# Three fused layers on one core: V's conversion, a second square tile, and the order of loads at a product's border

## The chip, the cores and the metric

The kernel runs on one core of a Trainium2 chip. Its engines are TensorE (PE, matmuls and weight loads), VectorE (DVE), ScalarE (ACT), GpSimd (POOL) and SyncE (SP, which here issues all DMA transfers). The metric is device time in microseconds (us). An engine executes its own instructions in order and waits on semaphores for the others.

## The reference

Three layers follow each other on 8 batches of 576 tokens with 512 channels.

```python
kv  = einsum('bhsd,bhse->bhde', k, v)            # attention without softmax, 8 heads of 64
out = einsum('bhsd,bhde->bhse', q, kv)
x   = out / sqrt(mean(out*out, -1) + 1e-6) * g_norm

u = x + (x^T @ U @ V)^T                          # U: 576 x 32, V: 32 x 576 (mixes tokens)
z = u + relu(u @ w_ch1) @ w_ch2                  # 512 -> 2048 -> 512

h = gelu(z @ w_in)                               # 512 -> 1024, halves hu and hv
result = z + (hu * (w_sg @ layernorm(hv) + b_sg)) @ w_out
```

The weights U, V, w_ch1, w_ch2, w_in and w_out arrive as 64-bit floats, and the kernel converts them on the chip.

## The kernel before, in words

**Numbers.** Products of the second and third layer run on fp32r halves: each operand is split into a high and a low part (`wh`, `wl`), and `three` (lines 346 to 349) issues three matmuls for one product. `convert` (lines 96 to 109) turns a 64-bit weight into fp32: two steps on ACT (lines 103, 104), three on DVE (106 to 108), one addition on POOL (109). These steps are marked `behind`: they keep their place in the program's order on their engine. `converted` (113) writes down the conversion, then flushes a queue of stores, then queues the store of its own result. A store (`split_to`, 123) is a copy on ACT (125) and a subtraction (126), on DVE for even blocks and on POOL for odd ones. So the store of block f is written down behind the conversion of block f + 1, unless `flush()` is called before.

**Order.** PE's order is the order of the code. The other engines and SP get a fixed order when the program is built: the framework's planner takes what it thinks is ready, and among that what comes first in the code; so an instruction that isn't `behind` can be put ahead of earlier ones, loads far ahead.

**Stage 1, per batch** (b = 0 to 7). `att_kv` multiplies K and V of the heads into a PSUM tile `kvps` (tag "ar", 4 buffers shared with `xps` and `ups`), `put_kv` copies it to `kvbd`. `att_x` (264) makes chunk c of 128 tokens: matmuls into `xps`, on ACT a square into the tile `sq` (276; one buffer) and a copy to `xn` (277), on DVE a sum of squares (278). `att_root` (281) is ten small DVE steps for the reciprocal root over all five chunks. `att_norm` (289) scales a chunk on DVE (295) and splits it into `xh` (ACT, 300) and `xl` (DVE, 301). `att_t` (304) multiplies with U into `tp`. `att_u` (321), for each quarter d of the channels, transposes the chunks (334) and multiplies with V's tile `v4` (336), both into `ups`, then scales the result (338, 340), stores it to `ud` in DRAM and splits it into `uh` and `ul` (343, 344). `ch1` (353) is one unit of the first product: 12 matmuls for half of a weight block f of 128 columns; 12 units per batch for blocks 0 to 5, whose outputs go to `yd` in DRAM. The other ten blocks are computed later in stage 1b by a scheme with seven products for eight (`Unit`).

**The head** (lines 470 to 522) prepares batches 0 and 1: loads; U's conversion; V's conversion in two halves, each followed by `store_v` (375: a copy on ACT, 376, and a subtraction on POOL, 377) into `v4`; then `att_kv(0)`, the five `att_x(0)`, root, `att_kv(1)`, the norms of batch 0 with its `att_t` and the `att_x` of batch 1 in between, `split_w(0)` and `split_w(1)`; then `att_u(0)`, the root and norms of batch 1 and `split_w(2)`, `split_w(3)`. Large tiles named `spare` stand in slots that the later coefficient tiles `c0` to `c4` will take.

**The periods** (524 to 571) run a list of steps per batch: U is a unit of `ch1`, X `att_x` and T `att_t` and D `att_u` of the next batch, K `att_kv` of the one after that. K0 and K1 are followed by the loads of that batch's third and fourth pair (`load_kv`, 165; tile `kvm` has 2 buffers, so a load waits for the K that last read its buffer). The first batch has a list of its own, `FIRST`.

**Stage 1b and the border** (575 to 713, then 716 on). The seven-product scheme runs over tokens in five blocks. Towards its end `load_w2` (682) loads the converted blocks of w_ch2 from DRAM (`wd`): blocks 8 to 15 into slots 0 to 7, which are free early, blocks 0 to 7 into a new pool `wb`, which lies where the tiles of stage 1b were.

**Stage 2, the second product** (773 to 807). 72 steps; a step takes 256 of the 2048 hidden channels of 512 tokens: `load_y` (743) loads `yr` from `yd` (one DMA) and makes relu and its low part (`yx`: ACT 752, DVE 753), then `ch2` issues 24 matmuls. Steps start with blocks 8 to 15, then 0 to 7; the input of the first two steps was loaded earlier (`y_at`). `load_z1` loads a batch of u for the residual.

Of the kernel before, what the change touches and what calls it, by code (L numbers as in the profile page):

```python
# [12 lines left out]
F32 = mybir.dt.float32  # L13
# [9 lines left out]
B, H, S, D = 8, 8, 576, 64  # L23
# [3 lines left out]
P = 128  # L27
# [32 lines left out]
def tile_kernel(ctx: ExitStack, tc: tile.TileContext, kvm, kvr, qt, gcol, uv, w12,  # L60
# [21 lines left out]
    def in_turn(*chains):  # L82

        end = object()
        while chains:
            chains = [steps for steps in chains if next(steps, end) is not end]
# [9 lines left out]
    def convert(raw, tmp):  # L96

        low, high = raw[:, :, 0], raw[:, :, 1]
        t = tmp.bitcast(I32)
        behind(nc.scalar.activation(tmp, high.bitcast(F32), AF.Abs))
        behind(nc.scalar.activation(low, low.bitcast(U32), AF.Copy, scale=2.0 ** -29))
        yield
        yield behind(nc.vector.tensor_scalar(tmp, tmp, 2.0 ** -15, 122879.9921875, ALU.max, ALU.min))
        yield behind(nc.vector.tensor_scalar(t, t, 3, 0x3FFFFFF8, ALU.logical_shift_left, ALU.bitwise_and))
        yield behind(nc.vector.scalar_tensor_tensor(t, high, -0x40000000, t, ALU.bitwise_and, ALU.bitwise_or))  # L108
        yield behind(nc.gpsimd.tensor_add(t, t, low))  # L109
# [9 lines left out]
    def flush():  # L119
        while queue:  # L120
            queue.pop(0)()
# [28 lines left out]
    def slot(i, shape, dt, name):  # L150

        return px["wa" if i < 14 else "xa"].tile([P] + shape, dt, tag=f"s{i}", name=f"{name}{i}")
# [49 lines left out]
    def split_w(f):  # L202
        w = slot(f, [2, DM], F32R, "w")
        wh[f], wl[f] = w[:, 0], w[:, 1]
        sub = nc.gpsimd if f % 2 else nc.vector
        converted(w_raw.pop((f, 0)), next_tmp(), split_to(w[:, 0], w[:, 1], sub))
# [39 lines left out]
    def att_kv(b, ps):  # L246
        if ps[0] == 0:
            at_s["kv", b] = pm.tile([P, NP, D], F32, tag="ar", bufs=4, name="kvps")
        acc = at_s["kv", b]
        for p in ps:  # L250
            m, r = kv_t.pop((b, p))
            for c in range(NC):
                src = m[:, c] if c < 4 else r
                for j in range(2):
                    mm(acc[j * D:(j + 1) * D, p, :], src[:, j * D:(j + 1) * D],
                       src[:, P + j * D:P + (j + 1) * D], start=(c == 0), stop=(c == NC - 1))
# [7 lines left out]
    def att_x(b, c):  # L264

        n = rows(c)
        if c == 0:
            at_s["ss", b] = small(b, "ss", 0)
            nc.gpsimd.memset(at_s["ss", b][64:, 4], 1.0)
        ps = pm.tile([P, H, D], F32, tag="ar", bufs=4, name="xps")  # L270
        for p in range(NP):
            mm(ps[:n, 2 * p:2 * p + 2, :], q_t[b, p][:, c * P:c * P + n], kvbd[:, p, :],  # L272
               start=True, stop=True)
        xn = xn_of(b, c)
        sq = ap.tile([P, H, D], F32, tag="sq", name="sq")
        nc.scalar.activation(sq[:n], ps[:n], AF.Square)
        nc.scalar.activation(xn[:n], ps[:n], AF.Copy)
        nc.vector.tensor_reduce(at_s["ss", b][:n, c], sq[:n], AX.X, ALU.add)
        at_s["x", b, c] = xn

    def att_root(b):
        ss = at_s.pop(("ss", b))
        y, t = (small(b, n, i) for i, n in ((1, "ny"), (2, "nt")))
        a, y2, t2 = (i.rearrange("p w h -> p (w h)") for i in (ss, y, t))
        nc.vector.tensor_scalar(a, a, 1.0 / D, EPS, ALU.mult, ALU.add)
        in_turn(rsqrt(y2, t2, a))
        at_s["y", b] = y

    def att_norm(b, cs):

        y = at_s["y", b]
        for c in cs:
            n = rows(c)
            xn = at_s["x", b, c]
            nc.vector.tensor_tensor(xn[:n], xn[:n], y[:n, c].unsqueeze(2).to_broadcast([n, H, D]),
                                    ALU.mult)
            xf = xn.rearrange("p h d -> p (h d)")
            xh = ap.tile([P, DM], F32R, tag="xh", bufs=2, name="xh")
            xl = xh[n:] if c == 4 else ap.tile([P, DM], F32R, tag="xl", bufs=2, name="xl")
            nc.scalar.activation(xh[:n], xf[:n], AF.Copy)  # L300
            nc.vector.tensor_sub(xl[:n], xf[:n], xh[:n].bitcast(F32))
            at_s["x", b, c] = xf, xh, xl
# [72 lines left out]
    def store_v(c, x):  # L375
        nc.scalar.activation(v4[:, c], x, AF.Copy)
        nc.gpsimd.tensor_sub(v4[64:96, c], x[64:96], v4[64:96, c].bitcast(F32))
# [104 lines left out]
    tmp_u = next_tmp()[:, :nu]  # L482
    in_turn(convert(uvr[0][:, :nu], tmp_u))
    store_u(tmp_u)
    tmp_v = [slot(i, [2, DM], F32, "tmpv")[:, 0, :HS] for i in (6, 7)]
    for h, (r, t) in enumerate(zip((uvr[0][:, nu:], uvr[1]), tmp_v)):
        in_turn(convert(r, t))
        store_v(slice(h * HS, (h + 1) * HS), t)
    att_kv(0, list(range(NP)))
    put_kv(0)  # L490
    for p in range(NP):
# [6 lines left out]
    for f in range(1, NA):  # L498
        load_w(f, 0)
    att_root(0)  # L500
    att_kv(1, list(range(NP)))
    put_kv(1)
    att_norm(0, (0, 1))
    for cs in ((0, 1), (2, 3), (4,)):
        if cs[0]:
            att_norm(0, cs)
        for c in cs:
            att_t(0, c)
        for c in cs:
            att_x(1, c)  # L510
        if cs[0] < 4:
            split_w(cs[0] // 2)
    for p in range(2):
        load_kv(2, p)
    for d in range(ND):
        att_u(0, d)
    att_root(1)
    for p in range(NP):
        load_q(2, p)
    split_w(2)  # L520
    att_norm(1, (0, 1))
    split_w(3)

    PERIOD = "X0 X1 X2 X3 U X4 U U K0 U K1 U T0 T1 U U T2 T3 U U T4 U K2 U K3 U D0 D1 D2 D3".split()
    FIRST = "U U U K0 U K1 U T0 T1 U U T2 T3 U U T4 U K2 U K3 U D0 D1 D2 D3".split()
    for b in range(B):
        n, n2 = (i if i < B else None for i in (b + 1, b + 2))
        i = 0
# [161 lines left out]
    while units:  # L690
        n = 3 if len(units) == 3 else 2
        two, units = units[:n], units[n:]
        a, b = two[0], two[-1]
        if n == 3:
            for s in "a5 a1 b5 b1 a3 a6 b3 b6 c5 c1 a7 b7 a2 c3 c6 b2 a4 c7 b4 c2 c4".split():
                two["abc".index(s[0])].product(int(s[1]))
                if s == "b7":
                    for f in range(12, 16):
                        load_w2(f)
        else:  # L700
            for x, p in ((a, 5), (a, 1), (b, 5), (b, 1), (a, 3), (a, 6), (b, 3), (b, 6), (a, 7), (b, 7),
                         (a, 2), (b, 2), (a, 4), (b, 4)):
                x.product(p)
        if b.j == len(BLOCKS) - 1 and b.i in (0, 1):
            y = up.tile([P, ND, S], F32, tag="u32", bufs=2, name="y0")
            y_at.append(y.rearrange("p d s -> p (d s)")[:, :2 * 2 * BT].rearrange("p (a f t) -> p a f t", a=2, f=2))
            for k in range(2):
                nc.sync.dma_start(y_at[0][:, k], yd[0][:, 8 + 2 * k:10 + 2 * k])
        if b.j == len(BLOCKS) - 1 and b.i == 1:
            for f in range(8, 12):  # L710
                load_w2(f)
    flush()
    pha.close()
# [25 lines left out]
    def load_z1(b):  # L739
        zt[b] = up.tile([P, ND, S], F32, tag="u32", bufs=2, name="z32")  # L740
        nc.sync.dma_start(zt[b], ud[b])
# [31 lines left out]
    steps = [(j, (i + 4) % 8) for j in range(NB) for i in range(8)]  # L773
    load_y(*steps[0])
    px["wb"] = wb = ph1.enter_context(tc.tile_pool(name="wb", bufs=1, side="left", reuse_waits="tile"))
    load_z1(0)
    load_y(*steps[1])
    for f in range(8):
        load_w2(f)
    for at_, (j, i) in enumerate(steps):  # L780
        if 2 <= at_ + 1 < len(steps):
            load_y(*steps[at_ + 1])
        step = at_ % 8
        if step == 0 and j + 1 < B:
            load_z1(j + 1)
        for k in range(2):
            ch2(j, 2 * i + k, step == 0 and k == 0, step == 7 and k == 1)
        if j == 0 and step == 5:
            raws = prepare_sg()
        if j == 1 and step < 5:  # L790
            split_sg(step, raws[step])
        if j == NB - 2 and step in (0, 1, 2, 3, 4, 5):
            if step == 0:
                load_wio(0)
            load_wio(step + 1)
            split_wio(step)
        if j == NB - 1:
            if 1 <= step < 7:
                if step < 6:
                    load_wio(step + 6)  # L800
                split_wio(step + 5)
            elif step == 7:
                flush()
            if step >= 3 and step < 7:
                split_z(0, step - 3, zt[order[0]][:, step - 3], nc.vector)
        if step == 7:
            z_out(j)
# [277 lines left out]
```

## Time and profile before

| | us |
|---|---|
| median of 3 runs (1394.03 to 1396.19) | 1395.4 |
| the profiled execution | 1394.67 |
| its span, first to last instruction | 1392.7 |
| PE busy | 1346.4 |
| DVE busy | 771.3 |
| ACT busy | 536.5 |
| POOL busy | 284.2 |

PE is busy for 97% of the span, with a mean granted clock of 0.992 of full speed. An operation's row gives its start, its duration, the engine, the line, output <- input and the shapes; a bracket gives the idle time of the engine ahead of it and who ended it. Rows of several instructions end in x and their number. Matmuls are pipelined, so their durations overlap; the distance of two starts is what one costs.

### The profile page before, as it was taken

The page shows a single profiled execution, that of the slowest core. Times are in us where ns is not written, and L with a number is a line of the kernel's source. Part 1 is how long each engine was busy: PE and PEld are TensorE (multiplying, and loading weights), DVE is VectorE, ACT ScalarE, POOL GpSimd, SP SyncE. Part 2 cuts the span into 40 slices and gives each one's busy share as a digit, 9 for nine tenths or more (in the row PEclk, how much of TensorE's full clock was granted, in tenths as well). Part 3 has the DMA queues.
Part 4 walks back from the last instruction along what each step waited for, and adds up shares of the span by engine and source line. Part 5 has one row for each costly group of instructions (what it writes and reads, how often), then busy time and mean ns, then how long its engine had stood idle before and what let it go on. Part 6 is the DMA issues. An engine that isn't in the chain of part 4 may idle for free.

```text
span 1392.7 us, 20749 instructions
## 1 busy us (share of the span) xinstructions
PE 1346.4 (97%) x8050; PEld 1177.5 (85%) x8050; DVE 771.3 (55%) x1405; ACT 536.5 (39%) x888; POOL 284.2 (20%) x268
## 2 busy tenths in 40 slices
PE   5799999999999999899999999999999999999998
PEld 4689999997777788688888888888999999999998
DVE  3757777755766732222322223456676775775874
ACT  3656656654554532212112122454333333423321
POOL 1211111100111100200000000336253453543332
PEclk9899999999999999999999999999999999999999
DMA  9556665355766777635434554631020120110001
GB/s 325 189 165 215 220 215 179 132 174 194 252 228 223 243 268 276 238 96 170 146 118 159 163 169 145 210 122 44 1 68 19 51 69 18 52 44 26 35 17 52
DMA packets 86930, 199.44 MB, mean 143 GB/s; under 512 B 12208, under 2 KB 33456, under 8 KB 85040
## 3 DMA queue, kind: packets, MB, share of 16 engines
q1 hardware_dynamic: 86832, 198.12, 42.9%
q8 instruction: 63, 1.03, 0.3%
q14 instruction: 35, 0.29, 0.1%
HBM read 126.00 MB, written 72.09 MB: 142 GB/s over the span
## 4 chain that ended last, share of the span: by engine, by line
PE 83%; DVE 5%; DMA 3%; ACT 2%; issue 1%; POOL 1%; SPq 0%; DVEq 0%; ACTq 0%; POOLq 0%
PE acc L348 9%; PE acc L347 9%; PE acc L349 9%; PE uso L936 8%; PE uso L957 6%; PE uso L848 5%; PE c L347 3%; PE c L348 3%; PE c L349 3%; PE y L347 3%; PE y L348 3%; PE y L349 3%; PE v L347 2%; PE v L348 2%; PE v L349 2%; PE xps L272 2%
## 5 line engine op out<-in xcount | busy, mean ns | idle before, releaser
L347 PE MATMUL acc<-yx,w 128*128 128x512 f32 x576 | 225.3, 391 | 5.9 <-ACT yx L752 5.9
L348 PE MATMUL acc<-yx,w 128*128 128x512 f32 x576 | 225.7, 392 | 1.5 <-DVE yx L753 1.5
L753 DVE SCALAR_TENSOR_TENSOR yx<-yr,yx 128x1024 fp32r<-128x1024 f32 x70 | 86.1, 1230 | 254.2 <-ACT yx L752 249.8
L349 PE MATMUL acc<-yx,w 128*128 128x512 f32 x576 | 225.3, 391 | 0.0
L752 ACT ACTIVATE yx<-yr 128x1024 fp32r<-128x1024 f32 x70 | 74.3, 1061 | 286.9 <-PE acc L349 267.0
L347 PEld LDWEIGHTS acc<-yx,w 128*128 128x128 f32 x576 | 108.8, 189 | 29.3 <-ACT yx L752 6.6
L348 PEld LDWEIGHTS acc<-yx,w 128*128 128x128 f32 x576 | 108.8, 189 | 24.7 <-DVE yx L753 2.1
L349 PEld LDWEIGHTS acc<-yx,w 128*128 128x128 f32 x576 | 108.9, 189 | 22.7
L349 PE MATMUL c<-uh,w 128*128 128x288 f32 x384 | 114.0, 297 | 6.6 <-POOL w L126 6.6
L347 PE MATMUL c<-uh,w 128*128 128x288 f32 x384 | 117.2, 305 | 0.0
L348 PE MATMUL c<-ul,w 128*128 128x288 f32 x384 | 114.1, 297 | 1.8 <-DVE ul L344 1.8
L848 PE MATMUL uso<-zh,wio 128*128 128x288 f32 x512 | 94.1, 298 | 0.8 <-DVE g2u L856 0.7
L957 PE MATMUL uso<-gh,wio 128*128 128x288 f32 x512 | 93.1, 296 | 0.0
L109 POOL TENSOR_TENSOR tmp<-tmp,wior 128x512 int32<-128x512 int32 x12 | 15.7, 1307 | 332.2 <-DVE tmp L108 287.2
L957 PEld LDWEIGHTS uso<-gh,wio 128*128 128x128 f32 x512 | 77.9, 188 | 2.3 <-issue 0.2
L347 PE MATMUL y<-T,c 128*128 128x512 f32 (+1 forms) x200 | 75.3, 377 | 4.0 <-DVE y L595 3.7
L848 PEld LDWEIGHTS uso<-zh,wio 128*128 128x128 f32 x512 | 76.3, 188 | 3.4 <-PE uso L936 1.4
L349 PEld LDWEIGHTS c<-uh,w 128*128 128x128 f32 x384 | 72.6, 189 | 7.1 <-POOL w L126 7.1
L348 PEld LDWEIGHTS c<-ul,w 128*128 128x128 f32 x384 | 72.6, 189 | 3.9 <-DVE ul L344 3.0
L347 PEld LDWEIGHTS c<-uh,w 128*128 128x128 f32 x384 | 72.5, 189 | 3.2 <-issue 1.0
L349 PE MATMUL y<-T,c 128*128 128x512 f32 (+1 forms) x200 | 74.5, 372 | 0.0
L348 PE MATMUL y<-T,c 128*128 128x512 f32 (+1 forms) x200 | 74.4, 372 | 0.0
(206 smaller groups left out, 2912.4 us busy)
## 6 DMA issues: line engine op xcount, KB each, us to landing
yr<-yd SPq DMA_DIRECT2D x70, 512.0 KB, 3.6
yd<-y SPq DMA_DIRECT2D x92, 256.0 KB, 3.5
kvm<-kvm_dram SPq DMA_DIRECT2D x28, 512.0 KB, 4.6
raw<-w_dram SPq DMA_DIRECT2D x26, 512.0 KB, 4.2
q<-qt_dram SPq DMA_DIRECT2D x32, 288.0 KB, 4.6
ud<-ut SPq DMA_DIRECT2D x32, 288.0 KB, 2.2
z<-ud SPq DMA_DIRECT2D x8, 1152.0 KB, 6.9
out_dram<-ot SPq DMA_DIRECT2D x31, 288.0 KB, 2.1
```

The costliest lines, as they stand in the source:

```text
L109: yield behind(nc.gpsimd.tensor_add(t, t, low))
L272: mm(ps[:n, 2 * p:2 * p + 2, :], q_t[b, p][:, c * P:c * P + n], kvbd[:, p, :], start=True, stop=True)
L347: mm(ps, ah, bh, start=start, stop=False, **kw)
L348: mm(ps, ah, bl, start=False, stop=False, **kw)
L349: mm(ps, al, bh, start=False, stop=stop, **kw)
L752: nc.scalar.activation(yh, y, AF.Relu)
L753: nc.vector.scalar_tensor_tensor(yl, y, 0.0, yh.bitcast(F32), ALU.max, ALU.subtract)
L848: mm(ps[:, e, :HS], a[:, s], c[:, halves[e]], start=(d == 0 and i == 0), stop=(d == ND - 1 and i == 2))
L936: mm(ps[:, e, :HS], a[:, s], w[:, halves[e]], start=(c == 0 and i == 0), stop=(c == NC - 1 and i == 1))
L957: mm(ops[d][:, e, :HS], a[:, s], c[:, f, halves[e]], start=(f == 0 and i == 0), stop=(f == ND - 1 and i == 2))
```

## The change

V's two conversions move from ahead of `att_kv(0)` to behind the norms of chunks 0 and 1 of batch 0, and run step by step side by side. Their stores move behind `split_w(1)`, followed by a `flush()`. The squares of batch 0 alternate between the tile `sq` and a free region of the tile `spare[4]`. `split_w(2)` and `split_w(3)` stand ahead of the root and norms of batch 1. In `FIRST`, K2 and K3 stand ahead of the T steps. At the border, blocks 14 and 15, the first `load_z1` and blocks 0 to 7 form a list; the first two are loaded at once, and then each step takes three from the list, behind its own `load_y`.

```diff
@@ att_x
         xn = xn_of(b, c)
-        sq = ap.tile([P, H, D], F32, tag="sq", name="sq")
+        if b or c % 2 == 0:
+            sq = ap.tile([P, H, D], F32, tag="sq", name="sq")
+        else:
+            sq = spare[4][:, 2700:2700 + DM].rearrange("p (h d) -> p h d", h=H)
@@ the head
     store_u(tmp_u)
-    tmp_v = [slot(i, [2, DM], F32, "tmpv")[:, 0, :HS] for i in (6, 7)]
-    for h, (r, t) in enumerate(zip((uvr[0][:, nu:], uvr[1]), tmp_v)):
-        in_turn(convert(r, t))
-        store_v(slice(h * HS, (h + 1) * HS), t)
     att_kv(0, list(range(NP)))
...
     att_root(0)
+    tmp_v = [slot(i, [2, DM], F32, "tmpv")[:, 0, :HS] for i in (6, 7)]
+    uv_in = [convert(r, t) for r, t in zip((uvr[0][:, nu:], uvr[1]), tmp_v)]
     att_kv(1, list(range(NP)))
     put_kv(1)
     att_norm(0, (0, 1))
+    in_turn(*uv_in)
     for cs in ((0, 1), (2, 3), (4,)):
...
         if cs[0] < 4:
             split_w(cs[0] // 2)
+        if cs[0] == 2:
+            for h, t in enumerate(tmp_v):
+                store_v(slice(h * HS, (h + 1) * HS), t)
+            flush()
...
     for d in range(ND):
         att_u(0, d)
+    split_w(2)
+    split_w(3)
     att_root(1)
     for p in range(NP):
         load_q(2, p)
-    split_w(2)
     att_norm(1, (0, 1))
-    split_w(3)
...
-    FIRST = "U U U K0 U K1 U T0 T1 U U T2 T3 U U T4 U K2 U K3 U D0 D1 D2 D3".split()
+    FIRST = "U U U K0 U K1 U K2 U K3 T0 T1 U U T2 T3 U U T4 U U D0 D1 D2 D3".split()
@@ the end of stage 1b
                 if s == "b7":
-                    for f in range(12, 16):
+                    for f in range(11, 14):
                         load_w2(f)
...
         if b.j == len(BLOCKS) - 1 and b.i == 1:
-            for f in range(8, 12):
+            for f in range(8, 11):
                 load_w2(f)
@@ the border
-    load_z1(0)
     load_y(*steps[1])
-    for f in range(8):
-        load_w2(f)
+    later_loads = [lambda f=f: load_w2(f) for f in (14, 15)] + [lambda: load_z1(0)] + [lambda f=f: load_w2(f) for f in range(8)]
+    later_loads.pop(0)()
+    later_loads.pop(0)()
     for at_, (j, i) in enumerate(steps):
         if 2 <= at_ + 1 < len(steps):
             load_y(*steps[at_ + 1])
+        for _ in range(3):
+            if later_loads:
+                later_loads.pop(0)()
```

## Rows read from the trace of the kernel before

**Rows 1.** Who waited for whom, PE: us in total, times, longest

```profile
PE c L349 <- POOL w L126: 6.6, 2, 6.2
PE acc L347 <- ACT yx L752: 5.9, 2, 4.5
...
PE tp L310 <- ACT xh L300: 5.6, 1, 5.6
```

**Rows 2.** Busy time in stretches, with the granted clock (PEclk) after POOL

```profile
31.70:52.71 21.01, 16.17 (x87) 12.30 (x87) 18.66 (x34) 16.27 (x31) 2.91 (x2) 0.87 0.55 193
...
61.38:64.00 2.62, 2.62 (x10) 2.42 (x10) 1.94 (x5) 1.74 (x3) 0.00 (x0) 0.50 0.05 20
...
565.30:570.00 4.70, 3.92 (x10) 2.94 (x11) 2.45 (x2) 1.74 (x2) 1.41 (x1) 0.64 0.47 141
570.00:650.00 80.00, 80.00 (x355) 66.20 (x354) 22.98 (x26) 17.88 (x19) 6.58 (x4) 1.00 0.44 140
```

**Rows 3.** Timeline of ACT: start us, us, operation; first and last square of batch 0

```profile
20.16 0.58 ACT L276 ACTIVATE sq<-xps 128x512 f32<-128x512 f32 x1
...
27.04 0.59 ACT L276 ACTIVATE sq<-xps 64x512 f32<-64x512 f32 x1 [0.32 <-DVE spare L278]
```

**Rows 4.** Timeline of PE, 21 to 28 us: the last matmuls of batch 0's chunks

```profile
20.76 1.63 PE L272 MATMUL xps<-kvbd,q 128*128 128x128 f32 x12
```

**Rows 5.** Timeline of all engines, 0 to 60 us: first tp, first matmul with V

```profile
33.11 0.79 PE L310 MATMUL tp<-xh,u 128*128 128x512 f32 x1 [5.58 <-ACT xh L300]
...
43.85 0.36 PE L336 MATMUL ups<-v,t 128*128 128x256 f32 x1 [1.21 <-DVE t L316]
```

**Rows 6.** V's conversion, the tile tmpv: ns min/median/max, first and last start

```profile
L106 DVE TENSOR_SCALAR tmpv<-tmpv x2: 310/480/651, 17.0 to 19.9; 128x288 f32<-128x288 f32 x2
L107 DVE TENSOR_SCALAR tmpv<-tmpv x2: 310/310/310, 17.3 to 20.6; 128x288 int32<-128x288 int32 x2
L108 DVE SCALAR_TENSOR_TENSOR tmpv<-uv,tmpv x2: 457/458/459, 17.7 to 21.0; 128x288 int32<-128x288 int32 x2
L109 POOL TENSOR_TENSOR tmpv<-tmpv,uv x2: 798/800/802, 18.3 to 21.6; 128x288 int32<-128x288 int32 x2
...
L377 POOL TENSOR_TENSOR v<-tmpv,v x2: 785/788/791, 19.6 to 23.0; 32x288 fp32r<-32x288 f32 x2
```

**Rows 7.** Timeline of all engines, 44 to 62 us: the wait for weight block 1

```profile
57.40 2.71 POOL L109 TENSOR_TENSOR tmp<-tmp,spare 128x512 int32<-128x512 int32 x1 [2.72 <-DMA raw<-w_dram]
...
60.07 1.25 POOL L126 TENSOR_TENSOR w<-tmp,w 128x512 fp32r<-128x512 f32 x1
...
61.38 0.61 PE L349 MATMUL c<-uh,w 128*128 128x288 f32 x1 [6.22 <-POOL w L126]
```

**Rows 8.** The tile kvm, 0 to 130 us: its 14 loads

```profile
DMA to landing us min/median/max: 3.4/4.6/10.6
```

**Rows 9.** Chain that ended last, in order of time: start us, us; K2, K3

```profile
81.57 0.88 PE kvps L255 x20
...
84.23 0.88 PE kvps L255 x20
```

**Rows 10.** Timeline of SP's queue at the border

```profile
545.72 0.43 SPq L685 DMA_DIRECT2D w<-wd  x1
...
546.70 3.35 SPq L685 DMA_DIRECT2D w<-wd  x7
...
551.10 4.19 SPq L748 DMA_DIRECT2D yr<-yd  x3
```

**Rows 11.** Timeline of PE at the border

```profile
560.41 0.39 PE L349 MATMUL acc<-yx,w 128*128 128x512 f32 x1
565.32 0.50 PE L347 MATMUL acc<-yx,w 128*128 128x512 f32 x1 [4.52 <-ACT yx L752]
...
569.66 0.40 PE L349 MATMUL acc<-yx,w 128*128 128x512 f32 x1
```

**Rows 12.** Timeline of DVE: the same pair of subtractions at two places

```profile
33.51 1.28 DVE L301 TENSOR_TENSOR xl<-spare,xh 128x512 fp32r<-128x512 f32 x2
...
70.58 2.69 DVE L301 TENSOR_TENSOR xl<-xn,xh 128x512 fp32r<-128x512 f32 x2 [1.00 <-ACT xh L300]
```

## The prediction, made before the changed kernel was run

> **What bounds the kernel now.** The profiled execution took 1394.67 us, of which the span is 1392.7; the median of the runs is 1395.4, so 0.7 is added to whatever the sum below gives. I read the waits of TensorE (PE) first. Three stand above the rest: 6.2 us for POOL's subtraction of a weight (line 126), 5.6 us for the first `xh` of batch 0 (line 300), and 4.5 us for the `yx` of a step of the second product (line 752) [rows 1]. Away from these places PE stands still nowhere for long: between 570 and 650 us, for example, it was busy for all 80.00 us [rows 2]. So what shortens one of the three waits shortens the run, unless another wait takes its place, and what is spent on another engine elsewhere costs nothing.
>
> The first wait in order of time lies in the head. PE ended the five chunks of batch 0's `xps` at 20.76 + 1.63 = 22.39 us [rows 4], but ScalarE (ACT) read the first chunk only at 20.16 and the last one at 27.04 [rows 3]. Ahead of the first stood both conversions of V, in program order on ACT; between the chunks stood the single `sq` tile, which VectorE (DVE) must have reduced before ACT may write the next square. From the last square to the first `tp` matmul the chain took 33.11 - 27.04 = 6.07 us [rows 3, 5]: reduction, reciprocal root, norm, `xh`.
>
> The second wait follows in the first period. The third unit of batch 0, the first that reads weight block 1, stood for 6.22 us before its third matmul, which came at 61.38, when POOL had made `wl[1]` at 60.07 + 1.25. POOL did this behind the addition of block 2's conversion, 57.40 to 60.11 [rows 7]: the store of block 1 is queued until the conversion of block 2 has been written down, so it stands behind it on POOL. The ten matmul rows after it lie in 2.62 us at a granted clock of 0.50, the lower level of 1.2 GHz [rows 2].
>
> The third lies at the border. Eight loads `w<-wd` were issued from 545.72 on, seven of them at 546.70 [rows 10], then one `z`, then the first `yr` at 551.10. PE finished what was resident with the matmul at 560.41 and went on at 565.32 [rows 11].
>
> **The change part by part.**
>
> Head, first part. V's ten steps on ACT, DVE and POOL leave the place ahead of the squares, and the chunks alternate between two `sq` tiles. Nothing is added in number: the second tile is a region of another tile, and the square there is the same instruction. ACT then follows PE: the last square can start where the last chunk ends, near 22.5 instead of 27.04, because ACT's square and copy of a chunk take about as long as PE's matmuls of the next. The chain of 6.07 behind it stays, so the first `tp` comes 4.5 us earlier, at about 28.6. V's work now lies behind the norms. On DVE it is 2 x (0.31 + 0.31 + 0.46) = 2.16 us [rows 6]; it waits for ACT's V steps, and the rest of the norms and the reductions of batch 1 are behind it. In the stretch from 31.70 to 52.71, which ends with the `ul` tiles that the units wait for, DVE was busy 18.66 of 21.01 us [rows 2]: 2.35 us are idle. If V fits there wholly, 4.5 are gained at the first unit; if none of it does, 2.3. The idle pieces are short and lie before waits for PE and ACT, some of which shrink as PE comes earlier; I take the middle, **-3.5**. V's two POOL additions and two subtractions, 2 x (0.80 + 0.79) = 3.18 us [rows 6], fall into time in which POOL has no weight to convert yet. V is needed by the `ups` matmuls, which came at 43.85 [rows 5] and would now come near 40; with ACT's V steps and the 2.16 on DVE before them, POOL's end near 28.6 + 1.4 + 2.2 + 3.2 = 35. That time covers them at no cost; if V slips by more than 5 us, `ups` waits for the rest. No DMA moves with V: its loads stay where they were.
>
> Head, second part. The `flush` behind `store_v` writes down the store of block 1 ahead of the conversions of blocks 2 and 3, and these stand ahead of the root of batch 1 on DVE and POOL. The wait of 6.2 goes; with it go 2.62 / 2 = 1.3 us that the half clock cost. By the rows of conversion and subtraction [rows 7] POOL needs about 1.6 + 1.25 for block 1, and starts when V is done; `wl[1]` is ready long before the third unit. What is late next is block 2: after the last `ul` it needs two conversions on DVE, POOL's two additions and a subtraction, about 5 us, and the unit that reads it stands behind three more units, K0 and K1, some 7 us. Bounds: 0 if another weight is late by as much, -7.5 if none is. I take **-7.5**, the near row being the wait itself.
>
> K2 and K3 stand earlier, so a new wait arises on PE. The load for K2 can go out on SP only when K0 has released its buffer. In between lie a unit, K1 and a unit. In the chain, one K and one unit repeat in 84.23 - 81.57 = 2.66 us, K itself taking 0.88 [rows 9], so the load has 2.66 + 1.78 = 4.4 us. The loads of `kvm` land 3.4 us after issue at best, 4.6 in the median and 10.6 at worst [rows 8], and the smaller `kvr` is issued behind it. So PE waits between 0 and 6.2; queued behind that wait are two units, K3 and the T steps, and everything that waits for them. K3's load goes out while K2 waits, so it is paid once. I take **+1.5**, by the median and the second issue. SP's loads for batch 3 go out earlier by the same move and have no reader in that stretch. `put_kv` of batch 2 on DVE moves too; its reader is a period away.
>
> Border. Now only two loads of weights and what is ready of `z` precede the `yr` of the third step; blocks 14 and 15 go to slots that have been free for long. On SP six of the eight issues that stood ahead of the first `yr` now stand behind it, and in the transfers six of eight loads less lie in front. In the old order eight weights, `z` and `yr` were in by 565.32 - 545.72 = 19.6 us, with the relu: at most 1.96 a load. The new `yr` is the third, so in near 552, the next the eighth (with `z`), 562, the third one the twelfth, 569; PE wants them at 560.6, and 5.4 and 10.8 us later (24 matmuls a step). So the 4.5 us go, and with them the second wait, for `yl`, and the half clock behind: without a stop the matmul at 569.66 is the ninth after 560.41 and would start 9 x 80.00 / 355 = 2.03 us after it, at 562.44 [rows 2, 11]. That is **-7.2**; the other end is 0. I take the full amount, as the margin is 2 us and more at every step.
>
> The sum is -3.5 - 7.5 + 1.5 - 7.2 = -16.7, so 1378.0 for that execution and, with the 0.7, about 1378.5 in the median.
>
> **Where a rule speaks against it.** Two of DVE's subtractions at line 301 took 1.28 us at 33.51, and 2.69 us at 70.58 [rows 12], where POOL was adding and subtracting; POOL's own addition took 2.71 at 57.40 [rows 7], against 0.80 for V's 288 columns with DVE mostly on reductions [rows 6]. So the two do hold each other up here. V's POOL steps are put from a quiet stretch into DVE's fullest one. By the forecast the DVE operations beside them are short or have one input, and nothing is added; if each POOL step holds DVE for its whole length, 3.2 us are, and the sum gives 1381.7. The Trainium skill, "SBUF — State Buffer", section "Who interferes with whom", says that DVE operations with two SBUF inputs and POOL operations that read SBUF exclude one another for the length of an instruction; by that rule the trace agrees at 70.58, and this rival is more than a guess.
>
> **The rivals.**
> - K2's load is late: 6.2 instead of 1.5, and an idle time of that length brought the half clock in this trace, 1.3 more. That is 6.0 on top: 1384.5. For it speaks the worst landing, against it the median, 4.6 [rows 8].
> - DVE and POOL hold each other up, as above: 1381.7.
> - The border stays: the issue order is a plan by priority, and if it still puts all eight weights first, 7.2 come back: 1385.7. Against it stands that the old plan kept `w`, `z`, `yr` in just the order of the code.
> - The change doesn't do what it says: ACT or DVE still has V ahead of the squares, and 3.5 come back: 1382. V's steps are kept in program order, which speaks against it.
> - Head and border both fail in full: no change.
> - Slower: PE falls to its lower clock for the twelve units of batch 0, because the new order feeds it in small pieces. Each us of PE work at half the clock adds one; a unit is 1.78, so more than nine of the twelve must run so before the gain of 16.7 is eaten, and with all twelve it is 21.4 more, 1399.9. Against it: the lower level came behind PE's waits of 4.5 us and more, and lasted few us [rows 2]; no wait of that length is left in the forecast.
>
> **How the numbers follow.** Forecast 0.52, late K2 0.15, DVE against POOL 0.12, border stays 0.10, V not moved 0.05, no change 0.03, half clock 0.03. A measurement of this kernel can tell about 0.2%, 2.8 us, from no change; all but the last two are faster by more: 0.94, 0.03, 0.03. The forecast's own range is 1374 to 1382: below, V hidden wholly (-1.0), no K2 wait (-1.5) and some of PE's smaller waits in the head; above, V wholly on the path and a longer K2 wait. To hold 8 in 10 it reaches to the two rivals near 1385: 1374 to 1386.
>
> **What would show it.** The first square of batch 0 near 18 us and the last near 22.5; the first `tp` near 28.6; no wait of PE for line 126; K2's matmuls with a DMA wait of 0 to 3 us; no wait of PE for `yx` at the third step of the border, and `yr` issued before the third of the eight weights. If PE waits as long as before for `wl` of another block, or `ups` for V, the second or the first step of the head is wrong; if `yr` still lands near 564, the border is.

## The result, and the profile of the changed kernel

The changed kernel took 1380.57 us in the median of 4 runs (1379.36 to 1381.29), the kernel before, measured beside it, 1395.80 (4 runs): ratio 0.9892, interval 0.9875 to 0.9909, so 15.2 us less, 12.7 to 17.4. The forecast was 1378.5, with 1374 to 1386 as its range. The profiled execution of the changed kernel took 1380.8 us, its span 1378.8, with a mean granted clock of 0.994 (before 0.992). Line numbers behind the edits are 3 or 6 higher in the rows shown: the square is L279, xh L303, tp L313 and L315, the units L350 to L352, yx L758.

The total is near the forecast, its parts are not. PE's timeline of the changed kernel, by its waits, with the first `ups` of batch 1 (81.52) as the mark at which the head ends:

```profile
27.27 0.79 PE L313 MATMUL tp<-xh,u 128*128 128x512 f32 x1 [1.99 <-ACT xh L303]
...
35.25 0.50 PE L313 MATMUL tp<-xh,u 128*128 128x512 f32 x1 [1.59 <-ACT xh L303]
...
48.79 0.40 PE L350 MATMUL c<-uh,w 128*128 128x288 f32 x1 [0.35 <-ACT uh L346]
...
50.18 0.48 PE L351 MATMUL c<-ul,w 128*128 128x288 f32 x1 [0.99 <-DVE ul L347]
...
67.48 1.12 PE L255 MATMUL kvps<-kvm 128*64 128x64 f32 x16 [2.49 <-DMA kvm<-kvm_dram]
...
81.52 0.38 PE L337 MATMUL ups<-ident,xn 128*128 128x128 f32 x2
```

The first `tp` comes 5.84 us earlier than in [rows 5]. The first unit, at 49.61 before, is only 0.82 earlier. The wait of 6.2 for `w` [rows 1] is gone, K2 doesn't wait, but K3 does. Batch 1's `ups`, at 86.74 before, is 5.2 earlier; the forecast for the head was 9.5. What took the lead of the first `tp` shows in the timelines of ACT, POOL and DVE, in this order:

```profile
21.97 0.60 ACT L279 ACTIVATE sq<-xps 64x512 f32<-64x512 f32 x1
...
33.48 0.44 ACT L379 ACTIVATE v<-tmpv 128x288 fp32r<-128x288 f32 x1 [4.23 <-POOL tmpv L109]
...
34.59 1.13 ACT L303 ACTIVATE xh<-spare 128x512 fp32r<-128x512 f32 x2
```
```profile
30.77 3.44 POOL L109 TENSOR_TENSOR tmpv<-tmpv,uv 128x288 int32<-128x288 int32 x2 [15.49 <-DVE tmpv L108]
```
```profile
30.90 1.88 DVE L298 TENSOR_TENSOR spare<-spare 128x512 f32<-128x512 f32 x3
```

V's copies stand in ACT's order ahead of `xh` of chunks 2 and 3 and wait 4.23 us for POOL. POOL starts at 30.77, behind V's last step on DVE, and its two additions take 3.44 together, against 0.80 each in [rows 6]: the first takes 2.68, the second 0.80. DVE's three norms of batch 0, with two inputs, lie beside the first, and 2.68 is its 0.80 plus their 1.88. So `xh` comes at 34.59, and the third chunk's `tp` at 35.25, which stood at 38.06 before.

What K3 waits for is seen in the timelines of DVE, ACT and SP, in this order; the last row is K3's load being issued:

```profile
59.90 1.89 DVE L298 TENSOR_TENSOR xn<-xn,ny 128x512 f32<-128x512 f32 x3
```
```profile
60.62 1.24 ACT L303 ACTIVATE xh<-xn 128x512 fp32r<-128x512 f32 x2 [1.09 <-DVE xn L298]
61.77 0.39 ACT L367 ACTIVATE y<-c 128x288 f32<-128x288 f32 x1
```
```profile
62.19 0.80 SPq L370 DMA_DIRECT2D yd<-y  x2
63.50 0.33 SPq L172 DMA_DIRECT2D kvm<-kvm_dram  x1
```

K1 had released the buffer at 60.5, but on SP the load stands behind the store of a unit's result, that store waits for ACT's copy, the copy stands behind batch 1's `xh`, and `xh` waits for DVE's norm. From 50 us on DVE has no time left (busy time of a stretch: PE, PEld, DVE, ACT, POOL, then clock):

```profile
50.00:65.50 15.50, 14.77 (x131) 13.07 (x131) 15.25 (x33) 9.66 (x19) 3.23 (x3) 0.89 0.66 215
```

The border lost its long wait, with one weight more ahead of `yr` than the prediction had. SP issues, against [rows 10], and PE behind its two short waits at 541.99 and 543.25 (1.42 and 0.76):

```profile
540.73 0.43 SPq L691 DMA_DIRECT2D w<-wd  x1
541.70 0.95 SPq L691 DMA_DIRECT2D w<-wd  x2
542.70 0.43 SPq L754 DMA_DIRECT2D yr<-yd  x1
543.17 0.53 SPq L691 DMA_DIRECT2D w<-wd  x1
...
545.25 0.38 SPq L754 DMA_DIRECT2D yr<-yd  x1
545.67 2.38 SPq L691 DMA_DIRECT2D w<-wd  x3
548.96 9.39 SPq L754 DMA_DIRECT2D yr<-yd  x3
```
```profile
547.00:556.00 9.00, 9.00 (x41) 7.47 (x40) 1.23 (x1) 1.38 (x2) 0.00 (x0) 1.00 1.03 420
556.00:570.00 14.00, 14.00 (x64) 11.59 (x63) 4.71 (x3) 5.85 (x8) 4.06 (x3) 1.00 0.94 365
```

Three of the eight weights (blocks 0 to 7) stand ahead of the first `yr`, not two, and `z` behind it. No PE wait is left behind the two short ones, and the clock stays whole. From the border's first matmul to the end of the span it is 836.8 us, before 845.7 (first matmul at 546.99): 8.9 less, where 7.2 were forecast.

### The profile page after: what moved, and what is told of

Its sections match the earlier page's. It is cut to its first block, busy times and chain, and to the rows that moved or that the text cites. A ratio compares the mean times of both kernels' runs of the same rounds, so it can differ in the third digit from the quotient of the medians.

```text
span 1378.8 us, 20740 instructions
## 1 busy us (share of the span) xinstructions
PE 1346.4 (98%) x8050; PEld 1178.8 (85%) x8050; DVE 772.4 (56%) x1405; ACT 535.8 (39%) x888; POOL 285.8 (21%) x268
## 4 chain that ended last, share of the span: by engine, by line
PE 82%; DVE 7%; DMA 3%; ACT 2%; issue 1%; POOL 1%; SPq 0%; DVEq 0%; ACTq 0%; POOLq 0%
PE acc L351 9%; PE acc L350 9%; PE acc L352 9%; PE uso L945 8%; PE uso L966 5%; PE uso L857 5%; PE c L350 4%; PE c L351 3%; PE c L352 3%; PE y L350 3%; PE y L351 3%; PE y L352 3%; PE v L350 2%; PE xps L272 2%; PE v L351 2%; PE v L352 2%
## 5 line engine op out<-in xcount | busy, mean ns | idle before, releaser
L350 PE MATMUL acc<-yx,w 128*128 128x512 f32 x576 | 224.2, 389 | 1.4 <-ACT yx L758 1.4
L352 PE MATMUL acc<-yx,w 128*128 128x512 f32 x576 | 224.1, 389 | 0.0
L758 ACT ACTIVATE yx<-yr 128x1024 fp32r<-128x1024 f32 x70 | 74.3, 1061 | 278.1 <-PE acc L352 257.9
L350 PEld LDWEIGHTS acc<-yx,w 128*128 128x128 f32 x576 | 108.1, 188 | 23.9 <-ACT yx L758 1.6
L352 PEld LDWEIGHTS acc<-yx,w 128*128 128x128 f32 x576 | 108.1, 188 | 22.6
L350 PE MATMUL c<-uh,w 128*128 128x288 f32 x384 | 117.4, 306 | 0.3 <-ACT uh L346 0.3
L352 PE MATMUL c<-uh,w 128*128 128x288 f32 x384 | 113.7, 296 | 0.0
L350 PE MATMUL y<-T,c 128*128 128x512 f32 (+1 forms) x200 | 75.3, 377 | 4.1 <-DVE y L601 3.6
L350 PEld LDWEIGHTS c<-uh,w 128*128 128x128 f32 x384 | 72.7, 189 | 3.9 <-issue 1.0
L352 PE MATMUL y<-T,c 128*128 128x512 f32 (+1 forms) x200 | 74.5, 372 | 0.0
L352 PEld LDWEIGHTS c<-uh,w 128*128 128x128 f32 x384 | 72.6, 189 | 0.0
```

The costliest lines, as they stand in the source:

```text
L350: mm(ps, ah, bh, start=start, stop=False, **kw)
L352: mm(ps, al, bh, start=False, stop=stop, **kw)
L758: nc.scalar.activation(yh, y, AF.Relu)
```

## The experiments

All twelve are read by the same marks. "First unit" is the start of the first matmul of the units of batch 0, "K0" and "ups" the first matmul of K0 in the first period and of batch 1's `ups`. "Border" is the time from the border's first matmul to the end of the span in the profiled execution; the median is of 4 to 12 runs. The kernel before was measured again beside each group of kernels; its medians lay between 1395.5 and 1396.1, and each ratio is against the one beside it. Two traces with the same head differ too: before and e1 by 1.2 us at the first unit and at K0, the changed kernel and e2 by 0.3 to 0.4 at the first three. So a shift of 1 us in a single trace says little.

| kernel | first unit | K0 | ups, batch 1 | border | median, us |
|---|---|---|---|---|---|
| before | 49.61 | 64.08 | 86.74 | 845.7 | 1395.8 |
| e1 border only | 48.42 | 62.88 | 86.88 | 836.4 | 1387.79 |
| e2 head only | 48.40 | 57.17 | 81.17 | 846.5 | 1389.74 |
| e3 flush only | 49.63 | 58.95 | 84.87 | 844.9 | 1393.67 |
| e5 flush, conversions, order | 50.07 | 58.22 | 81.57 | 846.9 | 1389.19 |
| changed kernel | 48.79 | 56.92 | 81.52 | 836.8 | 1380.57 |
| e4 V in front | 47.58 | 57.55 | 80.66 | 837.6 | 1381.88 |
| e6 flush later | 48.33 | 56.16 | 81.07 | 836.3 | 1380.92 |
| e7 V behind xh | 47.17 | 56.75 | 80.57 | 838.1 | 1381.25 |
| e8 V in front, flush later | 47.67 | 55.26 | 80.79 | 836.9 | 1380.72 |
| e9 K3 later | 49.38 | 57.73 | 81.03 | 837.9 | 1381.01 |
| e10 e8 with K3 later | 46.98 | 56.11 | 78.55 | 837.0 | 1380.67 |
| e11 K3 later, no first part | 49.28 | 58.66 | 80.95 | 837.2 | 1380.92 |
| e12 e10, block 3 flushed | 49.28 | 55.86 | 82.39 | 836.9 | 1382.39 |

**e1, the border alone.**

```diff
-                    for f in range(12, 16):
+                    for f in range(11, 14):
...
-    load_z1(0)
     load_y(*steps[1])
-    for f in range(8):
-        load_w2(f)
+    later_loads = [lambda f=f: load_w2(f) for f in (14, 15)] + [lambda: load_z1(0)] + [lambda f=f: load_w2(f) for f in range(8)]
...
```

> Before, with the border's part of the change alone. The prediction's term for it: 7.2 us under before. If the half clock that the old border shows at 549 to 552 us is caused by its waits, the trace of the changed kernel (8.9 us between the first matmul of the border and the end) is repeated: 8.5 to 9. If that half clock came by chance, 7.2 or a little less. If the border's gain depended on the new head (another phase of the stores and loads), under 5.

Ratio 0.9941 (0.9928 to 0.9954), 8.3 us under the 1396.12 of the kernel before. The gain doesn't need the new head. In its trace the border is 9.3 shorter than before's (836.4), in the median it is 8.3, between the two expectations of 7.2 and 8.5, and its interval (6.4 to 10.1 us) holds both. PE's waits there are 1.42 and 0.76 at 547.87 and 549.13, and none after.

**e2, the head alone** (the changed kernel with the old border).

```diff
-                    for f in range(11, 14):
+                    for f in range(12, 16):
...
```

> Before, with all of the change but the border's part. Theory of the trace: the head gave 5.2 us at the ups of batch 1, so 5 to 5.5 us under before, and the mark of the first matmul of the border 5.0 earlier. The prediction's sum: 9.5 (3.5 + 7.5 - 1.5). If head and border share something, their two gains don't add up to the 14.5 of the whole change.

Ratio 0.9952 (0.9939 to 0.9964): 6.4 less, not 9.5. With e1 that makes 14.7, against 15.2 for the whole: the two parts add up. The old border shows its wait in each trace that has it, at whatever time it comes: 4.52 before, 5.18 here, 3.55 in e3, 4.38 in e5.

**e3, the flush alone.**

```diff
             split_w(cs[0] // 2)
+        if cs[0] == 2:
+            flush()
```

> Before, with block 1's store flushed in front of the conversions of blocks 2 and 3, and nothing else. The prediction's term: the wait of 6.2 us for wl goes, with 1.3 of half clock: 7.5 us under before, more than the whole head gives. If the store's steps on ACT get in front of uh here too, the units start later by 1 to 2 and 5 to 6 stay. Rival: the wait only moves to the next block's weights (blocks 2 and 3, converted later here than in the changed kernel) or to K2's load, and 0 to 3 stay.

Ratio 0.9981 (0.9971 to 0.9990), 2.5 us. The rival held. The wait of 6.22 for block 1 is gone and comes back at blocks 2 and 3; PE's timeline:

```profile
63.98 0.40 PE L349 MATMUL c<-uh,w 128*128 128x288 f32 x1 [0.95 <-DVE w L126]
70.63 0.45 PE L349 MATMUL c<-uh,w 128*128 128x288 f32 x1 [2.28 <-POOL w L126]
```

**e5, the flush with the conversions of blocks 2 and 3 moved ahead and the new order** (V, the squares and the border as before).

```diff
+        if cs[0] == 2:
+            flush()
...
+    split_w(2)
+    split_w(3)
     att_root(1)
...
-    split_w(2)
     att_norm(1, (0, 1))
-    split_w(3)
...
-    FIRST = "U U U K0 U K1 U T0 T1 U U T2 T3 U U T4 U K2 U K3 U D0 D1 D2 D3".split()
+    FIRST = "U U U K0 U K1 U K2 U K3 T0 T1 U U T2 T3 U U T4 U U D0 D1 D2 D3".split()
```

> Before, with the second part of the head alone: the flush, both conversions of blocks 2 and 3 ahead of the root of batch 1, and the new order of the first period. The flush alone gave 2.5 us, as the waits for wl came back at the blocks converted later (0.95 and 2.28 us in its trace, one with half clock). Theory: the conversions moved ahead are what the flush lacked, so no PE wait for the weights is left, and the mark of batch 1's ups stands 4 to 5 us earlier than before (86.74); 4 to 5 under before. If the prediction's term is right: 6 (7.5 less 1.5). If two squares and V are needed for it too: 2 to 3.

Ratio 0.9957 (0.9942 to 0.9972): 6.4 us, as much as the whole head of e2, though its first `tp` stands at 32.25 and that of e2 at 25.98. So the first part of the head (V and the two squares) is worth nothing that these runs can tell, and the second part is worth the 6.0 forecast for it. The earlier conversions and the new order of the first period went in together here; what each is worth was not tried. No PE wait for a weight is left; K3 waits:

```profile
68.28 0.69 PE L255 MATMUL kvps<-kvm 128*64 128x64 f32 x16 [1.64 <-DMA kvm<-kvm_dram]
```

**e4, V back in front.**

```diff
     store_u(tmp_u)
+    tmp_v = [slot(i, [2, DM], F32, "tmpv")[:, 0, :HS] for i in (6, 7)]
+    for h, (r, t) in enumerate(zip((uvr[0][:, nu:], uvr[1]), tmp_v)):
+        in_turn(convert(r, t))
+        store_v(slice(h * HS, (h + 1) * HS), t)
...
-    in_turn(*uv_in)
...
-            for h, t in enumerate(tmp_v):
-                store_v(slice(h * HS, (h + 1) * HS), t)
```

> The changed kernel with V's conversion and store back in front of the norms; two squares, flush, order of the first period and border kept. My theory: V's move gains 5.8 us at the first tp and gives nearly all of it back, as V's copies stand in front of xh of chunks 2 and 3 on ACT and wait for POOL; so this kernel is within 1.5 us of the changed one at the end, on either side, with its first tp near 32 to 33 and no wait of ACT for V between the chunks. The prediction's term: V in front costs 2.3 to 3.5 us more than the changed kernel. If V's new place is a loss by itself: 1 to 3 us less than the changed kernel.

Ratio 0.9899 (0.9885 to 0.9914), beside 0.9892 for the changed kernel: no difference that can be told. The first `tp` comes 2.56 later (29.83), the third chunk's 0.26 later (35.51), the first unit 1.21 earlier (47.58). The first `tp` was expected at 32 to 33; it comes earlier, as the two squares stay in this kernel. What V's move gains at the first `tp` it has all but lost by the third. The 1.21 are lost again before K0 (57.55, in the changed kernel 56.92): the three units up to there run at a mean granted clock of 0.66, in the changed kernel at 0.79.

**e7, V's store behind the split of chunks 2 and 3.**

```diff
-        nc.scalar.activation(v4[:, c], x, AF.Copy)
+        behind(nc.scalar.activation(v4[:, c], x, AF.Copy))
...
             att_norm(0, cs)
+        if cs[0] == 2:
+            for h, t in enumerate(tmp_v):
+                store_v(slice(h * HS, (h + 1) * HS), t)
...
-            for h, t in enumerate(tmp_v):
-                store_v(slice(h * HS, (h + 1) * HS), t)
```

> The changed kernel with V's store behind the split of chunks 2 and 3, so that V's copies stand behind xh on ACT. Theory: xh no longer waits for POOL, the third chunk's first tp comes at 31 to 33 instead of 35.25; if nothing else takes its place, the first unit comes 2 to 3 earlier. Rival: the head is then bound by V itself or by DVE, as in the kernel with V in front (first unit 47.58 against 48.79), and 0 to 1 is gained. If K3's load sets the time at 67, nothing is seen at the end.

The third chunk's `tp` comes at 31.84 instead of 35.25, with no wait for `xh`, so V's copies on ACT were what held it (in e2, with the head of the changed kernel, it stands at 33.95):

```profile
31.84 0.48 PE L313 MATMUL tp<-xh,u 128*128 128x512 f32 x1
```

The first unit comes 1.62 earlier, between the 2 to 3 of the theory and the 0 to 1 of the rival, and the end is where it was: ratio 0.9896 (0.9881 to 0.9911). Of the 1.62 only 0.17 is left at K0: the units up to there run at a mean granted clock of 0.57 (0.79 in the changed kernel) and take 9.58 us instead of 8.13. Then K2 waits 1.72 for its load, and K3 stands at 67.23 (67.48 in the changed kernel).

**e6, the flush behind batch 0's ups.**

```diff
-            flush()
...
         att_u(0, d)
+    flush()
```

> The changed kernel with the flush behind batch 0's ups, so that ACT's store of block 1 stands behind all uh. Theory: PE's waits of 0.35 and 0.99 us ahead of the first unit and the half clock behind them (50 to 53.5 us) go, the first units end 2 to 2.5 us earlier; at the end 1 to 2.5 under the changed kernel. Rival: block 1's weights then come late, and PE waits for wl at the third unit, so nothing or a loss of 1 to 3. Second rival: the load of K3 sets the time at 67 and all of the gain is swallowed there: 0.

Ratio 0.9897 (0.9881 to 0.9913). The second rival held at the end. The first unit no longer waits for `uh`, but the half clock behind it stayed (0.58 from 50 to 53.5 us, in the changed kernel 0.55). K0 is 0.76 earlier (56.16); K3, which waits for its load, is 0.53 earlier, batch 1's `ups` 0.45, and in the median nothing is left:

```profile
66.95 0.69 PE L255 MATMUL kvps<-kvm 128*64 128x64 f32 x16 [2.72 <-DMA kvm<-kvm_dram]
```

**e8, V in front and the flush later** (the edits of e4 and e6).

> The kernel with V in front (its trace: half clock 0.64 from 50 to 58, batch 1's ups at 80.66) with the flush behind batch 0's ups as well. Theory: 1 to 2.5 under the kernel with V in front, batch 1's ups at 78.5 to 80, the best so far. Rival: weights late at the third unit, 0 to 3 more. Second rival: K3's load swallows it.

Ratio 0.9894 (0.9878 to 0.9911). The second rival held again: K0 stands at 55.26, with the clock at 1.00 from 50 to 58 us, and K3's wait has grown to 3.44, K3 at 66.77. In e4 to e8 and the changed kernel K3 stands between 66.77 and 68.28, whatever came before, and batch 1's `ups` 13.3 to 14.1 behind it.

**e9, K3 later in the first period.**

```diff
-    FIRST = "U U U K0 U K1 U K2 U K3 T0 T1 U U T2 T3 U U T4 U U D0 D1 D2 D3".split()
+    FIRST = "U U U K0 U K1 U K2 U T0 T1 U U K3 T2 T3 U U T4 U U D0 D1 D2 D3".split()
```

> The changed kernel with one edit to the first period's order: K3 stands behind T0 T1 and two units more instead of ahead of them. Theory: K3's load, not the head, sets the time at 67 us, whatever comes before; with 6 us more of work ahead of it the DMA wait of 2.49 and the half clock behind it (0.76) go, batch 1's ups come at 78.3 to 79.5 instead of 81.52, and the end is 2 to 3.2 lower. Rival: the units that take K3's place need weights that POOL stores at 68.2 only, PE waits for those instead, and 0 to 1.5 is gained, or a loss.

Ratio 0.9890 (0.9873 to 0.9906), 1381.01: the rival held. K3 no longer waits, but a unit does, for block 3's low half:

```profile
68.84 0.40 PE L352 MATMUL c<-uh,w 128*128 128x288 f32 x1 [1.84 <-POOL w L126]
```

**e10, the same edit on e8.**

> The kernel with V in front, two squares and the flush behind batch 0's ups, with K3 two units later too. Its K0 stood at 55.26, the earliest of all, and its K3 wait was 3.44. Theory: batch 1's ups at 77 to 78, 3 to 4 less at the end than without the edit, about 1376.5 to 1378. Rival: the weights bind, and it ends within 1 of the changed kernel.

Its profiled execution, 1378.35, is the lowest of the four (up to 1381.41), with batch 1's `ups` at 78.55; its median is 1380.67, ratio 0.9886 (0.9870 to 0.9902). So the mark moved in one execution, and the median didn't. That trace tells why the weights are late (POOL):

```profile
63.80 1.30 POOL L109 TENSOR_TENSOR tmp<-tmp,spare 128x512 int32<-128x512 int32 x1 [5.56 <-issue]
65.06 1.26 POOL L126 TENSOR_TENSOR w<-tmp,w 128x512 fp32r<-128x512 f32 x1
```

The subtraction of block 3 (65.06) had its inputs when ACT's copy ended at 59.95 + 0.62 = 60.57, but stands behind the addition of block 4's conversion, which waits for DVE's line 108 (62.99 + 0.67). It is the pattern of block 1 in the kernel before, two blocks on.

**e11, K3 later, V in front, one square.**

> The changed kernel with V in front and one square (none of the first part of the head), and K3 two units later. Under the theory that K3's load hid what the first part of the head gives, the first part shows now: K0 stood 1.3 later without it (58.22 against 56.92), so this kernel ends 1 to 1.5 above the changed kernel with K3 later. If the two end within 0.5, the first part is swallowed by something else too (weights, or the store of the conversions).

1380.92 (1379.62 to 1382.15) against 1381.01 (1380.41 to 1381.25) for e9, measured together: the two are alike, so the first part is swallowed with K3 out of the way too. Block 3's low half sets the time in both: the unit that waits for it goes on at 68.84 in e9 and here, though K0 stands 0.93 later, at

```profile
68.77 0.40 PE L349 MATMUL c<-uh,w 128*128 128x288 f32 x1 [0.85 <-POOL w L126]
```

**e12, block 3 flushed as well,** on e10.

```diff
     split_w(3)
+    flush()
```

> The kernel with V in front, two squares, the flush behind batch 0's ups and K3 later, with block 3's store flushed too, right behind its conversion. In the trace without this edit POOL's last step of block 3 had its inputs at 60.6 but stood behind block 4's addition (63.80) and ran at 65.06 to 66.32; PE waited 1.01 for it. Theory: both gates of the stage (K3's load and block 3's weights) are then gone, POOL's step runs near 60, no PE wait between 52 and 70 us, batch 1's ups at 77.0 to 78, and the end 1 to 3 under the kernel without the edit (median 1380.67, profiled 1378.35). Rival: the next thing late takes its place (block 4's weights, or xl of batch 1, which a wait of 0.16 already shows), and nothing is gained.

The rival held: 1382.39, ratio 0.9907 (0.9892 to 0.9922), no better than e10. POOL's subtraction runs at 60.23, no unit waits for it, and the next thing is late: `xl` of batch 1, from a DVE that is full. Its timelines of DVE and PE, and its windows:

```profile
58.26 4.08 DVE L298 TENSOR_TENSOR xn<-xn,ny 128x512 f32<-128x512 f32 x3
```
```profile
70.89 0.50 PE L315 MATMUL tp<-xl,u 128*128 128x512 f32 x1 [1.32 <-DVE xl L304]
...
72.90 0.80 PE L315 MATMUL tp<-xl,u 128*128 128x512 f32 x1 [0.79 <-DVE xl L304]
```
```profile
58.00:67.00 9.00, 9.00 (x91) 8.21 (x90) 8.96 (x13) 4.52 (x9) 3.89 (x3) 1.00 0.52 170
```

The three norms took 4.08 us, against 1.89 in the changed kernel, with POOL's addition and subtraction (57.98, 60.23) beside them. Half clock follows: 0.72 in the mean of 67 to 79 us. None of these kernels beats the changed kernel by more than its runs scatter.

## Why the prediction was right in the sum, and where its steps failed

**The border, -7.2: right, a little undersized.** 8.3 in e1 (6.4 to 10.1, so the medians alone don't tell it from 7.2); in the traces the border took 844.9 to 846.9 us in the four with the old order and 836.3 to 838.1 in the ten with the new one, some 8.9 less. The wait, its second part and the half clock behind them went as the step said, though `yr` was issued ahead of the fourth weight and not of the third: the margin held that too. Most of the rest is a half clock that the old border shows behind its first two short waits as well: the granted clock was at 0.50 somewhere between 544 and 552 us in all four traces with the old border that the table has (before, e2, e3, e5), and in two of ten with the new one (e7, e9, whose border is the longest of the ten, by some 1.2 us). The step took the rows at 560 and behind and left that one out. Whether the old order causes it or it came by chance isn't settled: the two short waits, 1.42 and 0.76, are the same in both orders.

**The head's second part, -7.5 and +1.5: right in its sum.** e5 gave 6.4 (3.9 to 8.1) for the 6.0 of the two terms. The step named the flush and the earlier conversions together; e3 shows that the flush alone is worth 2.5, as the wait moves on to blocks 2 and 3. With their earlier conversion and the earlier K2 and K3 it stays away; which of the two does it wasn't tried. The wait of the +1.5 came at K3, not at K2: 2.49 us, with a clock of 0.52 for some 3.5 us behind it. "K3's load goes out while K2 waits" was wrong: on SP the load stood behind a store that waited for ACT.

**The head's first part, -3.5: failed, no gain can be told** (6.4 in e5 and in e2, and 0.1 between e11 and e9). The squares did what was said (last one 21.97, forecast 22.5; first `tp` 27.27, forecast 28.6, of which 0.5 is U's conversion, which started earlier in this execution). Then two things went wrong. First, the step found room for V on DVE and called its POOL steps free, and it left V's copies on ACT out, which are queued ahead of `xh`; they waited 4.23 us, 1.5 until POOL could start and 2.7 for its first addition. "Short or have one input" was wrong of the DVE operations beside it: they were the norms, with two. The rival "DVE and POOL hold each other up" priced 3.2 us on DVE's side, while the cost fell on POOL and on ACT behind it. The rule that the prediction weighed, in the Trainium skill, "SBUF — State Buffer", section "Who interferes with whom", speaks of just such a pair, a DVE operation with two SBUF inputs and a POOL operation that reads SBUF. The trace agrees with it: 2.68 us for an addition of 0.80. Second, and this decides: even with that mended (e7) or with V in front (e4, e8), the lead is nearly gone by 67 us (batch 1's `ups` 0.7 to 1.0 before the changed kernel's), and none shows in the medians. In e4 and e7 PE's own lower clock took most of it before K0; in e8 it was K3's wait. The step counted DVE's idle time up to 52.71; the stretch that sets the head's end is the one behind it, where DVE has the roots and norms of batch 1, the `ul` tiles and two conversions, and was busy 15.25 of 15.50 us (up to the issue of K3's load 11.9 of 12.5 us in e4, 11.9 of 12.6 in e7 and 12.4 of 12.5 in e8, from 50 us on). K3's load, block 3's weights and `xl` of batch 1 come late one behind the other, so close together that taking one away (e9, e12) puts the next in its place: that is shown. That all three hang on the full DVE is read from the rows of the changed kernel, e10 and e12. By this reading less work on DVE there would show at the end; that was not tried.

So the forecast came out 2.1 us low. The parts measured alone, 8.3, 6.4 and nothing, make 14.7 of the 16.7: 3.5 too much for the first part, less 1.1 and 0.4 too little for the border and the second part. The whole gave 15.2, 0.5 more than its parts, which the scatter covers, and the median of the kernel before was 0.4 above the 1395.4 that the forecast started from. That a sum with one term of 3.5 worth nothing came so near is in part luck: two other terms erred the other way. The rivals "border stays" and "half clock for the twelve units" didn't come; the clock was low for part of the units only (0.79 from 50 to 58 us).

## What to carry to other kernels

When a wait is taken out of a stage, look at the engine that is busiest in the stage behind it: where several things come late one behind the other, a lead won ahead of them can be lost there. Here it was, in every order that was tried. A step that is moved takes a place in every in-order queue that it passes; here two copies of 0.44 us made ACT stand for 4.2 us ahead of `xh`, and a load on SP was late because the store ahead of it waited for a copy two engines away. Test the parts of a change one by one and in sums: a total that fits hid one part that was worth nothing.

## What the hardware did that was not expected

POOL's work stretched DVE's smallest operations most in proportion: two root steps of 128x40 (L93) took 1.31 and 1.33 us beside POOL's additions, and 0.20 elsewhere. Both ended within 0.1 us of POOL's addition, at 55.92 and 58.93 against 55.86 and 58.87. The timelines of POOL and DVE in the changed kernel:

```profile
57.11 1.76 POOL L109 TENSOR_TENSOR tmp<-tmp,spare 128x512 int32<-128x512 int32 x1 [1.25 <-ACT w L125]
```
```profile
57.60 1.33 DVE L93 SCALAR_TENSOR_TENSOR nt<-nt,ss 128x40 f32<-128x40 f32 x1
...
59.43 0.20 DVE L93 SCALAR_TENSOR_TENSOR nt<-nt,ss 128x40 f32<-128x40 f32 x1
```

And TensorE's clock fell behind short waits, where the prediction looked for it behind waits of 4.5 us and more. The trace of the kernel before had this already: 0.50 from 550 to 552 us, behind waits of 1.42 and 0.76. In the changed kernel it was 0.53 from 26 to 33 us, behind waits of 1.99 and 0.76. Behind the border's waits of 1.42 and 0.76 it was 1.00 in the changed kernel and fell to 0.50 in e7, with the same matmuls; why it falls in one execution and not in the other stays open:

```profile
544.00:546.00 2.00, 2.00 (x6) 1.54 (x5) 0.00 (x0) 0.00 (x0) 0.00 (x0) 0.50 1.04 424
```
